# A finer first normalisation, a bias loaded element by element and a memset moved, in a two-layer attention and MLP kernel

## Chip, cores and metric

The kernel runs on one core of a Trainium2 chip. The metric is the device time of one execution in microseconds (us), measured several times; the median is quoted, with the lowest and highest. The profile is of one of these executions. Its span (first to last instruction) is about 2 us shorter than the device time. The "granted clock" is the share of its full clock at which TensorE was let run; 1.000 is all of it.

## The reference, cut to what matters

The program is two layers of attention and MLP on x of 2048 tokens by 1024 channels, in bf16. The biases b1 and b2 are the same in both layers.

```python
# attention: 32 heads of 32, each token looks at 8 keys, 2 apart (0, 2, ..., 14 tokens back)
x = x + attention(layernorm(x), wqkv, wo)      # wqkv: 1024 x 3072, wo: 1024 x 1024
x = x + gelu(layernorm(x) @ w1 + b1) @ w2 + b2 # w1: 1024 x 3584, w2: 3584 x 1024, b1: 3584
x = x + attention(layernorm(x), wqkv, wo)
x = x + gelu(layernorm(x) @ w1 + b1) @ w2 + b2
```

## The kernel before

Tokens are handled in four groups of 512 (4 tiles of 128). For each group the kernel computes queries, keys and values chunk by chunk on TensorE, with VectorE doing the attention products beside it. Order on TensorE is fixed by the program. Weights come through a pool of five 1 MB tiles; SyncE issues the weight loads and the DMA transposes of the normalised x in program order, and GpSimd issues a few others. "K(0)" below is the key phase of group 0 (units 8 to 15 of the first stage), and "V(0)" the value phase behind it.

The start: the first two x tiles are normalised and transposed on TensorE, and the first query matmuls need the transposed columns 0 to 255 of both.

```python
def norm(tt, parts=1):
    rstd = lnp.tile([P, 1], F32, name="rstd")
    vec.reciprocal(rstd[:], stds[tt][:])
    xn = lnp.tile([P, D], BF16, name="xn", bufs=3)
    for h in range(parts):
        cols = slice(h * D // parts, (h + 1) * D // parts)
        vec.tensor_scalar(out=xn[:, cols], in0=x[tt][:, cols], scalar1=mvs[tt][:, 0:1], scalar2=rstd[:],
                          op0=ALU.subtract, op1=ALU.mult)
    return xn

stats(0)
stats(1)
xn0 = norm(0)
xn1 = norm(1, 2)                       # 512 columns, then 512
transpose_on_pe(xn0, xa[0][:, 0, :, :], parts=[act.copy] * 4)
transpose_on_pe(xn1, xa[0][:, 1, :, :], parts=[vec.tensor_copy] * 2, k1=KD // 2)
transpose_on_pe(xn1, xa[0][:, 1, :, :], parts=[act.copy] * 2, k0=KD // 2)
# ... cut: statistics of the next tiles
```

The biases: b1 is wanted with its 3584 values spread over partitions (`b1T[p, j] = b1[j * 128 + p]`), for the ScalarE GELU. It is read as 28 rows of 128 and transposed on TensorE in K(0). b2 is read as one row of 2 KB, repeated on all 128 partitions.

```python
b1_rows = attp.tile([KF, P], BF16, name="abc")                      # KF = 28
pool.dma_start(b1_rows[:], B_b1.rearrange("(j p) -> j p", p=P))     # at the very start

def load_b2():
    pool.dma_start(b2bc[:], B_b2.unsqueeze(0).to_broadcast([P, D]))

def transpose_bias():
    ps = psum.tile([P, KF], BF16, name="acc", bufs=8)
    pe(nc.tensor.transpose(ps[:], b1_rows[:], ident[:KF, :KF]))
    act.copy(b1T[:], ps[:])
# ... cut
stage(gen_qkv(0, qk_next=early), sides=at(8, transpose_bias) + at(9, ln_stats_ahead, 2, NTT - 2)
      + at(11, ln_end) + at(14, load_b2))
q1 = gen_qkv(1, defer=True, qk_pool=early, mix=NCH // 2)
stage(q1, sides=at(0, gather, 0) + at(11, between, 0, 1) + at(11, hold) + each(av, 0, 12, 1))
```

`at(u, f)` calls f after unit u. `ln_end` normalises the last two tiles of group 2 and sends them through two DMA transposes; the SyncE queue then holds, in this order: the query weights of group 1 and the first half of its key weights, those two transposes, the second half of the key weights ("the second key-weight half" below), the value weights. The second half must take the buffer of V(0)'s first value-weight half.

## Time and profile before

| | before |
|---|---|
| device time, median of 3 (lowest to highest) | 1230.99 us (1230.79 to 1232.06) |
| profiled span | 1228.7 us |
| TensorE busy | 1223.1 us |
| waits of TensorE after 8.6 us | none |

The page gives busy time, share of the span and number of instructions of each engine (its part 1), and the shares of the chain of work that ended last, followed back from the last instruction (its part 4). PE is TensorE's matmuls, PEld its weight loads, DVE VectorE, ACT ScalarE, POOL GpSimd, SP SyncE.

```profile
PE 1223.1 (100%) x5771; PEld 632.5 (51%) x5771; DVE 862.1 (70%) x913; ACT 319.2 (26%) x515; POOL 108.7 (9%) x211
...
PE 99%; DVE 0%; DMA 0%; issue 0%
```

TensorE is the whole chain. The list of waits of TensorE (who waited for whom: total us, times, longest) says how little there is to take away:

```profile
PE acc L220 <- DVE xn L92: 1.5, 1, 1.5
PE acc L117 <- DVE big L92: 1.0, 1, 1.0
PE acc L117 <- DVE xnT L92: 0.2, 1, 0.2
```

All three lie in the first 8.6 us. In order of time (start us, length us, what), the chain shows the two places that the change aims at: the 12 transposes and the copy ahead of the first matmul, and at 25.32 the bias transpose.

```profile
7.12 0.93 PE acc L220 x12
...
8.08 0.30 DVE xnT L92
...
8.52 4.13 PE acc L117 x36
...
25.32 0.12 PE acc L181
```

The timeline (start us, length us, engine, line, operation, out<-in, and in brackets the idle time before and what ended it):

```profile
25.36 0.59 ACT L92 CAST kT<-acc 128x512 bf16<-128x512 f32 x1 [1.35 <-PE acc L117]
...
27.35 0.59 ACT L92 CAST kT<-acc 128x512 bf16<-128x512 f32 x1 [1.32 <-PE acc L117]
...
41.08 0.63 POOL L92 DMA_DIRECT2D b2bc<-in_B_b_dram  x1
...
43.50 9.31 SPq L92 DMA_TRANSPOSE xnT<-qT  x2
...
52.90 1.08 SPq L92 DMA_DIRECT2D wt<-in_A_wqkv_dram  x2
...
54.84 1.07 ACT L92 CAST qT<-acc 128x512 bf16<-128x512 f32 x2 [2.09 <-DMA xnT<-qT]
...
60.16 0.59 ACT L92 CAST kT<-acc 128x512 bf16<-128x512 f32 x1 [1.14 <-PE acc L117]
```

The two DMA transposes are landed by 54.84 (the query copy waits for them, because it reuses the memory that they read). The load at 52.90 is the second key-weight half; taken by itself, the trace gives its time from issue to landing:

```profile
DMA to landing us min/median/max: 5.6/5.6/5.6
```

So it lands at 52.9 + 5.6 = 58.5 us. TensorE wants it half a chunk after the four query chunks, near 59.3 us: about 0.8 us of slack. In windows (PE, PEld, DVE, ACT and POOL busy us, then the granted TensorE clock, the busy share of the DMA engines and GB/s), TensorE is full, and up to 60 us the DMA engines are full too. (Their share sums the times of all packets, and packets overlap, so it can exceed 1.)

```profile
50.00:55.00 5.00, 5.00 (x25) 3.31 (x24) 4.97 (x3) 1.70 (x5) 0.00 (x0) 1.00 1.20 197
55.00:60.00 5.00, 5.00 (x25) 3.34 (x24) 4.93 (x4) 2.09 (x4) 0.00 (x0) 1.00 1.00 377
60.00:65.00 5.00, 5.00 (x25) 3.33 (x24) 5.00 (x3) 1.76 (x3) 2.17 (x4) 1.00 0.32 122
```

A packet is one entry of the trace's DMA records: one piece moved by one engine.

### The profile page before, as it was taken

Reading aid. Unit: us, or ns where it says so; the run is one execution under the profiler, and the core shown is the slowest. Engines: PE = TensorE matmul, PEld = TensorE weight load, DVE = VectorE, ACT = ScalarE, POOL = GpSimd, SP = SyncE. Lnnn points to the kernel's source line nnn. Section 1 sums busy time; section 2 is a strip of 40 time slices with the busy share of each in tenths; the row PEclk is TensorE's granted clock in tenths of the full one; section 3 lists DMA queues with packets and bytes.
Section 4 is the critical chain, followed back from the end, with each engine's and each line's share of the span. In section 5 each row is a group of like instructions: output and inputs, shape, how many; then the busy total and the mean of one; then the engine's idle time right before and its main releaser. Section 6 shows DMA issues by size and latency. Waiting matters only on the chain.

```text
span 1228.7 us, 14007 instructions
## 1 busy us (share of the span) xinstructions
PE 1223.1 (100%) x5771; PEld 632.5 (51%) x5771; DVE 862.1 (70%) x913; ACT 319.2 (26%) x515; POOL 108.7 (9%) x211
## 2 busy tenths in 40 slices
PE   9999999999999999999999999999999999999999
PEld 7666544456444564446544465444654444444444
DVE  7999887998997999375993759937599797011001
ACT  5443253014310244202441024410244001400310
POOL 2310014010101101100001000000000002000000
PEclk9999999999999999999999999999999999999999
DMA  9954665766638645856557565576664568446441
GB/s 298 294 205 157 180 204 182 201 173 204 218 128 244 187 150 167 237 171 177 157 161 229 171 171 179 159 215 202 171 201 146 187 194 209 148 160 195 156 134 53
DMA packets 220031, 226.64 MB, mean 184 GB/s; under 512 B 68194, under 2 KB 187136, under 8 KB 217920
## 3 DMA queue, kind: packets, MB, share of 16 engines
q1 hardware_dynamic: 214704, 208.69, 56.7%
q0 software_dynamic: 5264, 17.06, 3.6%
q8 instruction: 45, 0.74, 0.3%
q14 instruction: 18, 0.15, 0.0%
HBM read 189.01 MB, written 4.19 MB: 157 GB/s over the span
## 4 chain that ended last, share of the span: by engine, by line
PE 99%; DVE 0%; DMA 0%; issue 0%
PE acc L117 99%; DMA x<-in_A_x_dram 0%; DVE stats L92 0%; PE acc L220 0%; DVE xn L92 0%; DVE x L92 0%; DVE mv L92 0%; DVE xnT L92 0%; PE acc L181 0%; DVE rstd L92 0%
## 5 line engine op out<-in xcount | busy, mean ns | idle before, releaser
L117 PE MATMUL acc<-xnT,wt 128*128 128x512 bf16 (+1 forms) x3392 | 720.5, 375 | 0.2 <-DVE xnT L92 0.2
L117 PEld LDWEIGHTS <-wt 128*128 128x128 bf16 x3392 | 400.7, 120 | 317.6 <-issue 0.3
L117 PE MATMUL acc<-wt,hT 128*128 128x512 bf16 (+1 forms) x1820 | 388.1, 376 | 0.0
L117 PEld LDWEIGHTS <-hT 128*128 128x128 bf16 x1820 | 178.1, 98 | 209.0
L92 DVE TENSOR_TENSOR big<-big 128x1024 bf16<-128x1024 bf16 (+2 forms) x184 | 244.9, 1360 | 2.2
L92 ACT ACTIVATE hT<-acc,b1T 128x512 bf16<-128x512 f32 x224 | 152.0, 688 | 322.2 <-PE acc L117 322.1
L92 DVE TENSOR_TENSOR big<-qT,kT 128x4096 bf16<-128x4096 bf16 x64 | 143.9, 2284 | 38.8 <-ACT kT L92 35.8
L92 DVE TENSOR_TENSOR big<-abc,vT 128x4096 bf16<-128x4096 bf16 x64 | 144.7, 2285 | 11.3 <-DMA abc<-a 9.2
L92 DVE TENSOR_TENSOR tmp<-acc,b2bc 128x512 f32<-128x512 f32 x56 | 38.6, 690 | 157.3 <-PE acc L117 154.3
L92 ACT CAST qT<-acc 128x512 bf16<-128x512 f32 (+1 forms) x72 | 38.2, 545 | 277.8 <-PE acc L117 275.7
L117 PE MATMUL acc<-wt,oT 128*128 128x512 bf16 x448 | 97.8, 379 | 0.0
L92 DVE BATCH_NORM_STATS2 stats<-x 128x6 f32<-128x512 bf16 x116 | 77.5, 682 | 6.1 <-DMA x<-in_A_x_dram 5.1
L117 PEld LDWEIGHTS <-oT 128*128 128x128 bf16 x448 | 43.9, 98 | 52.8
L92 DVE TENSOR_TENSOR x<-acc,big 128x512 bf16<-128x512 f32 (+1 forms) x9 | 5.7, 633 | 90.0 <-PE acc L117 90.0
L92 ACT CAST vT<-acc 128x512 bf16<-128x512 f32 x64 | 37.5, 586 | 100.8 <-PE acc L117 100.8
L92 POOL TENSOR_TENSOR rstd<-mv,eps_t 128x1 f32<-128x1 f32 x54 | 16.7, 310 | 530.1 <-DVE mv L92 530.1
L92 ACT CAST kT<-acc 128x512 bf16<-128x512 f32 x64 | 37.4, 585 | 64.6 <-PE acc L117 64.6
L92 DVE TENSOR_TENSOR x<-acc,x 128x512 bf16<-128x512 f32 x64 | 43.0, 672 | 4.6 <-PE acc L117 4.2
L92 DVE TENSOR_SCALAR xn<-x,mv,rstd 128x1024 bf16<-128x1024 bf16 (+1 forms) x53 | 28.6, 542 | 20.1 <-POOL rstd L92 19.7
L92 DVE TENSOR_TENSOR x<-tmp,x 128x512 bf16<-128x512 f32 x56 | 38.6, 690 | 1.4
L92 POOL DMA_DIRECT2D big<-big x24 | 13.3, 564 | 212.6 <-DVE big L92 212.5
L92 ACT ACT_TABLE_LOAD x17 | 21.8, 1283 | 36.6 <-DVE e L92 28.4
(64 smaller groups left out, 276.6 us busy)
## 6 DMA issues: line engine op xcount, KB each, us to landing
wt<-in_B_w_dram SPq DMA_DIRECT2D x56, 1024.0 KB, 5.7
wt<-in_B_w_dram SPq DMA_DIRECT2D x64, 896.0 KB, 4.9
wt<-in_A_wqkv_dram SPq DMA_DIRECT2D x46, 1024.0 KB, 5.6
wt<-in_A_wo_dram SPq DMA_DIRECT2D x16, 1024.0 KB, 5.1
abc<-a POOLq DMA_DIRECT2D x32, 256.0 KB, 5.1
big<-big POOLq DMA_DIRECT2D x24, 256.0 KB, 3.8
x<-in_A_x_dram SPq DMA_DIRECT2D x16, 256.0 KB, 7.1
out_dram<-x SPq DMA_DIRECT2D x31, 128.0 KB, 1.8
```

What stands on the lines that cost most here:

```text
L92: inst = f(*args, **kwargs)
L117: return pe(nc.tensor.matmul(*args, **kwargs))
```

## The change

Intent: let the first matmul start sooner (only 256 columns of the second tile have to be normalised and transposed first), take the bias transpose off TensorE by letting the DMA write b1 in transposed order with the cast to float32, and relieve GpSimd of one memset. The core of the diff:

```diff
+    vec.memset(zhalo[:], 0.0)
...
     def build_constants():
-        pool.memset(zhalo[:], 0.0)
...
-    b1_rows = attp.tile([KF, P], BF16, name="abc")
-    pool.dma_start(b1_rows[:], B_b1.rearrange("(j p) -> j p", p=P))
+    def load_b1():
+        pool.dma_start(b1T[:], B_b1.rearrange("(j p) -> p j", p=P))
...
-    def transpose_bias(): ...
...
-        def norm(tt, parts=1):
+        def norm(tt, bounds=(0, D)):
...
-            for h in range(parts):
-                cols = slice(h * D // parts, (h + 1) * D // parts)
+            for lo, hi in zip(bounds[:-1], bounds[1:]):
+                cols = slice(lo, hi)
...
-        xn1 = norm(1, 2)
+        xn1 = norm(1, (0, 2 * P, D))
-        transpose_on_pe(xn1, xa[0][:, 1, :, :], parts=[vec.tensor_copy] * 2, k1=KD // 2)
-        transpose_on_pe(xn1, xa[0][:, 1, :, :], parts=[act.copy] * 2, k0=KD // 2)
+        transpose_on_pe(xn1, xa[0][:, 1, :, :], parts=[vec.tensor_copy], k1=2)
+        transpose_on_pe(xn1, xa[0][:, 1, :, :], parts=[vec.tensor_copy] + [act.copy] * 2, k0=2)
...
-sides=at(8, transpose_bias) + at(9, ln_stats_ahead, 2, NTT - 2) + at(11, ln_end) + at(14, load_b2)
+sides=at(9, ln_stats_ahead, 2, NTT - 2) + at(11, ln_end) + at(13, load_b1) + at(14, load_b2)
```

More of the change, by code (lines that the diff above doesn't have):

```diff
@@ L170, in build_constants @@
         pool.dma_start(mask[0::NTT, :, :], first[:])
-    b1_rows = attp.tile([KF, P], BF16, name="abc")
-    pool.dma_start(b1_rows[:], B_b1.rearrange("(j p) -> j p", p=P))
+    def load_b1():
+        pool.dma_start(b1T[:], B_b1.rearrange("(j p) -> p j", p=P))
     def load_b2():
         pool.dma_start(b2bc[:], B_b2.unsqueeze(0).to_broadcast([P, D]))
-    def transpose_bias():
-        ps = psum.tile([P, KF], BF16, name="acc", bufs=8)
-        pe(nc.tensor.transpose(ps[:], b1_rows[:], ident[:KF, :KF]))
-        act.copy(b1T[:], ps[:])
     def ln_stats(t, mv=None, rstd=None):
@@ L629 @@
         load_x(1)
-        stage(gen_qkv(0, qk_next=early), sides=at(8, transpose_bias) + at(9, ln_stats_ahead, 2, NTT - 2) + at(11, ln_end) + at(14, load_b2))
+        stage(gen_qkv(0, qk_next=early), sides=at(9, ln_stats_ahead, 2, NTT - 2) + at(11, ln_end) + at(13, load_b1) + at(14, load_b2))
         q1 = gen_qkv(1, defer=True, qk_pool=early, mix=NCH // 2)
```

## The prediction

> **What bounds the kernel now.** The chain of waits is TensorE for 99% of the 1228.7 us span; TensorE is busy 1223.1 us. Its waits are three, all before 8.6 us: 1.5 us for the first normalised tile, 1.0 us for the warm-up data, 0.2 us for the transposed tile. From 8.52 us on it waits for nothing, so the change can gain only before 8.52 us or by removing TensorE work, and can lose by making TensorE wait.
>
> **Gain 1, start-up.** In the chain, 12 PE transposes (7.12 to 8.06 us) lead to VectorE's copy at 8.08, and that to the first matmul at 8.52. Eight are tile 0's; four are the second tile's first 512 columns, of which only two must now precede the first copy. In the timeline transposes issue about 0.065 us apart: 0.13 us saved. VectorE's second normalisation still ends near 7.91 us (estimated from 512 columns at 0.41 and 1024 at 0.55 us), so the copy can start near 7.95. The other six transposes run from 7.96 to about 8.36. The first matmul should start at 8.38 to 8.42.
>
> **Gain 2.** The bias transpose holds 0.12 us of the chain at 25.3 us; it goes, with an off-chain 0.19 us ScalarE copy.
>
> **No effect.** The zhalo memset took 0.21 us on GpSimd; VectorE is idle from 0.92 to 3.53 us. The early b1 load (7 KB) is negligible.
>
> **Cost: the new b1 load.** It moves 3584 elements of 2 bytes with a cast. The Trainium skill ("DMA: Bandwidth & Descriptors", Rules for kernel authors) says that a non-contiguous last dimension becomes one descriptor per element and that a cast must be issued from GpSimd; no run shows it yet. That is about 224 tiny packets per DMA engine. In the trace's packet records a 4-byte packet took 9 ns, a 256-byte one 18 ns: an estimated 2 to 4 us of all 16 engines, issued near 41 us, where the DMA share is about 1.0 (windows, 40 to 60 us). GpSimd must also produce the descriptors: perhaps 10 to 25 us, a guess.
>
> b1T is first read at 156 us. Three others have deadlines: the second key-weight half of group 1, issued at 52.9 behind two DMA transposes, wanted near 59.3, landing near 58 (slack about 1 us, the thinnest); gather(0) on the GpSimd queue, issued at 62.6, landing near 67, read at 71.0; behind it VectorE's attention of group 0, ready roughly 2 to 4 us before its output projection at 123.9. I expect the tiny packets to drain before 55 us: probably no stall.
>
> **Prediction.** 1230.99 - 0.12 - 0.12 = 1230.75 without a stall (about two chances in three); with a stall of 0.5 to 5 us otherwise, 1230.9 us overall, range 1230.0 to 1234.0. Faster by over 2%: 0.005; within 2%: 0.97; slower by over 2%: 0.025.
>
> **What would show it right.** First 256-column matmul near 8.40 us; no 28x28 transpose; TensorE's waits still all before 9 us; a GpSimd issue of b1T near 41 us longer than the 0.63 us of b2's; about 3600 more packets on the software queue; gather(0) issued by 63 us.
>
> **What would make it wrong.** A TensorE wait for weights at 59 to 62 us, or at the output projection near 124 us (gather(0) late, VectorE slipped). Or an unmoved first matmul: the six late transposes end last. A gain over 0.5 us would mean that the early b1 load had delayed the x tiles.

## More of the kernel before

The two key copies on ScalarE at 25.36 and 27.35 follow two chunks of eight matmuls; the bias transpose lies between them.

In the microsecond from 53 to 54 the DMA queues (packets, MB, share of 16 engines) held one entry, the transposes' 256-byte packets:

```profile
q1 hardware_dynamic: 1152, 0.29, 127.8%
```

## The result, and the profile after

| | before | after |
|---|---|---|
| device time, median of 6 (lowest to highest) | 1231.06 us (1230.79 to 1232.06) | 1235.63 us (1233.69 to 1237.22) |
| ratio, after over before | | 1.0036, 95% interval 1.0023 to 1.0049 |
| profiled span | 1228.7 us | 1231.5 us |
| mean granted clock over the six runs | 1.000 (in every later run listed) | 1.000, 0.999, 0.999, 0.997, 1.000, 0.998 |

Ratios are the mean time of one kernel's runs over that of the other's runs of the same rounds, so not quite the ratio of the medians quoted. The change made the kernel slower by some 4.6 us, well within 2%, but outside the predicted range. The profiled execution happens to be the quickest of the six (1233.69 us), so its loss of 2.8 us is the least of it.

The page after, parts 1 and 4 as above:

```profile
PE 1221.0 (99%) x5720; PEld 632.5 (51%) x5770; DVE 862.2 (70%) x914; ACT 318.8 (26%) x514; POOL 115.1 (9%) x210
...
PE 95%; DMA 2%; DVE 2%; issue 1%; SPq 0%; POOL 0%; DVEq 0%
```

The chain is no longer TensorE alone. (The smaller count of matmuls is of records missing from the trace; the weight loads fell by the one that was removed.) The list of waits names the newcomer at once:

```profile
PE acc L117 <- DMA wt<-in_A_wqkv_dram: 2.9, 1, 2.9
PE acc L117 <- DVE big L92: 1.0, 1, 1.0
PE acc L213 <- DVE xn L92: 0.9, 1, 0.9
```

The timeline after, cut to the lines that answer to those shown before:

```profile
7.22 1.35 PE L213 MATMUL acc<-ident,xn 128*128 128x128 bf16 x16 [0.92 <-DVE xn L92]
8.43 4.19 PE L117 MATMUL acc<-xnT,wt 128*128 128x256 bf16 x36
...
25.33 0.58 ACT L92 CAST kT<-acc 128x512 bf16<-128x512 f32 x1 [1.35 <-PE acc L117]
27.06 0.58 ACT L92 CAST kT<-acc 128x512 bf16<-128x512 f32 x1 [1.14 <-PE acc L117]
...
40.85 1.65 POOL L92 DMA_DIRECT2D b1T<-in_B_b_dram  x1
...
42.50 0.59 POOL L92 DMA_DIRECT2D b2bc<-in_B_b_dram  x1
...
43.34 8.27 SPq L92 DMA_TRANSPOSE xnT<-qT  x2
...
51.70 1.09 SPq L92 DMA_DIRECT2D wt<-in_A_wqkv_dram  x2
...
59.37 2.05 ACT L92 CAST qT<-acc 128x512 bf16<-128x512 f32 x4 [6.92 <-DMA xnT<-qT]
...
61.84 13.39 PE L117 MATMUL acc<-xnT,wt 128*128 128x512 bf16 x61 [2.87 <-DMA wt<-in_A_wqkv_dram]
...
62.96 0.59 ACT L92 CAST kT<-acc 128x512 bf16<-128x512 f32 x1 [1.54 <-PE acc L117]
```

Three copies on ScalarE measure where the time went. The first key copy of K(0) moved from 25.36 to 25.33 us: in this pair of profiles the start-up part had gained 0.03 us by then. The second moved from 27.35 to 27.06: the distance between the two fell from 1.99 to 1.73 us, so the bias transpose had cost TensorE 0.26 us (in load_only, below, the distance is 1.73 us too, and in start_only, which kept the bias transpose, 2.00). The first key copy of group 1 moved from 60.16 to 62.96: 2.80 us late, which is also the difference of the spans. Everything is decided by 63 us; the stall cost 2.80 + 0.29 = 3.1 us, of which the wait itself is 2.87.

The second key-weight half was issued 1.2 us earlier than before (51.70 against 52.90), yet took almost twice as long to land:

```profile
DMA to landing us min/median/max: 10.1/10.1/10.1
```

It landed at 61.8 us. It stands in the SyncE queue behind the two DMA transposes, and these were landed only at 59.37 instead of 54.84 us. In the same microsecond, 53 to 54, the queues show why:

```profile
q1 hardware_dynamic: 383, 0.10, 125.7%
q0 software_dynamic: 385, 0.00, 76.8%
```

The transposes moved 383 packets instead of 1152, and beside them passed 385 packets with hardly a byte in them: b1's elements, on GpSimd's queue. One for one. (This is the last part of the transposes. Before it they differed little: from the first transpose packet to 53 us, 787 packets in 2.4 us in the kernel before, 1095 in 3.7 us in the changed one.) The windows show the hole in TensorE, and in the first line a DMA share that is up and a GB/s that is down by half:

```profile
50.00:55.00 5.00, 5.00 (x25) 3.34 (x24) 4.97 (x4) 1.25 (x4) 0.00 (x0) 1.00 2.00 109
55.00:60.00 5.00, 3.97 (x19) 2.37 (x17) 4.93 (x4) 0.63 (x2) 0.00 (x0) 1.00 1.38 222
60.00:65.00 5.00, 3.16 (x15) 2.14 (x16) 3.29 (x2) 2.32 (x5) 2.16 (x4) 1.00 0.98 364
```

The trace's packet records add a second suspect. Before, b2's load (64 packets of 4096 bytes) went through from 45.1 to 47.2 us. After, it stood behind the elements in GpSimd's queue and went through from 54.2 to 58.5 us, on the end of the transposes; single packets of it took up to 1.47 us, against at most 0.44 us before.

### The profile page after: what moved, and what is told of

It reads as the page before. It is cut to its first block, busy times and chain, and to the rows that moved or that the text cites. A ratio compares the mean times of both kernels' runs of the same rounds, so it can differ in the third digit from the quotient of the medians. Undisturbed runs are those within 1.5% of the kernel's fastest.

```text
span 1231.5 us, 13954 instructions
## 1 busy us (share of the span) xinstructions
PE 1221.0 (99%) x5720; PEld 632.5 (51%) x5770; DVE 862.2 (70%) x914; ACT 318.8 (26%) x514; POOL 115.1 (9%) x210
## 3 DMA queue, kind: packets, MB, share of 16 engines
q0 software_dynamic: 8832, 17.07, 4.3%
## 4 chain that ended last, share of the span: by engine, by line
PE 95%; DMA 2%; DVE 2%; issue 1%; SPq 0%; POOL 0%; DVEq 0%
PE acc L117 95%; DMA wt<-in_A_wqkv_dram 1%; DVE big L92 1%; DMA x<-in_A_x_dram 1%; SPq L92 0%; DVE stats L92 0%; DVE qT L92 0%; POOL rstd L92 0%; DVE mv L92 0%; DVE x L92 0%; DVEq L92 0%
## 5 line engine op out<-in xcount | busy, mean ns | idle before, releaser
L92 DVE TENSOR_SCALAR xn<-x,mv,rstd 128x1024 bf16<-128x1024 bf16 (+2 forms) x53 | 28.6, 540 | 20.0 <-POOL rstd L92 19.8
```

Of the source, the lines that this page charges most:

```text
L92: inst = f(*args, **kwargs)
```

## The experiments

Theory A: the 3584 element packets alternate, packet by packet, with SyncE's queue on the DMA engines, draw out the transposes, and so delay the second key-weight half. Rival B: any cast load by GpSimd at this moment, ahead of b2's, does it, whatever its packets. Rival C: the new start-up shifts everything by 0.3 us and that uses up the slack. More theories came as runs fell out otherwise than expected. All runs gave correct results except where said.

Medians are of 4 to 6 runs; "before" is the kernel before in the same rounds. "Wait" is TensorE's total wait for key or query weights in the profiled execution.

| run | median us (lowest to highest) | before | ratio, 95% interval | wait us |
|---|---|---|---|---|
| load_only | 1236.03 (1232.71 to 1236.45) | 1231.22 | 1.0033 (1.0020 to 1.0045) | 3.7 |
| start_only | 1231.05 (1230.62 to 1231.91) | 1231.22 | 0.9999 (0.9985 to 1.0012) | none |
| load_late | 1230.70 (1230.52 to 1231.52) | 1231.22 | 0.9997 (0.9984 to 1.0009) | none |
| contiguous | 1230.79 (1230.41 to 1231.14) | 1231.22 | 0.9995 (0.9983 to 1.0008) | none |
| half_load | 1231.80 (1230.79 to 1232.40) | 1231.21 | 1.0005 (0.9992 to 1.0017) | none |
| double_load | 1232.29 (1231.76 to 1233.11) | 1231.21 | 1.0009 (0.9996 to 1.0023) | 1.8 |
| keys_first | 1237.34 (1236.42 to 1239.96) | 1231.21 | 1.0056 (1.0044 to 1.0069) | 0.2, and 5.6 for ScalarE |
| sync_queue | 1232.51 (1231.96 to 1234.18) | 1231.21 | 1.0015 (0.9999 to 1.0030) | 1.7 |
| b2_first | 1233.09 (1232.48 to 1234.50) | 1230.98 | 1.0019 (1.0006 to 1.0031) | 3.3 |
| b2_late | 1232.23 (1230.52 to 1232.42) | 1230.98 | 1.0006 (0.9993 to 1.0018) | 1.5 |
| b2_shifted | 1230.68 (1230.44 to 1232.40) | 1230.98 | 0.9999 (0.9985 to 1.0013) | none |
| after_again | 1237.10 (1235.27 to 1238.20) | 1230.98 | 1.0046 (1.0033 to 1.0059) | 4.8 |
| b2_rows | 1234.04 (1232.06 to 1237.14) | 1231.04 | 1.0031 (1.0019 to 1.0044) | 1.3 |
| b2_shifted_more | 1231.40 (1230.46 to 1232.15) | 1231.04 | 1.0001 (0.9988 to 1.0015) | 0.6 |

### Which part of the change: load_only and start_only

load_only is the kernel before with the new load alone; start_only is the changed kernel with the old b1 path put back.

```diff
 load_only, against the kernel before:
-    b1_rows = ...; pool.dma_start(b1_rows[:], ...); def transpose_bias(): ...
+    def load_b1(): pool.dma_start(b1T[:], B_b1.rearrange("(j p) -> p j", p=P))
-sides=at(8, transpose_bias) + ... + at(14, load_b2)
+sides=... + at(13, load_b1) + at(14, load_b2)
 start_only, against the changed kernel: these lines the other way round
```

> The kernel before with the new b1 load alone (element DMA at its new place, no bias transpose; 512+512 normalisation and the GpSimd memset kept). Theory A (the 3584 two-byte packets share the DMA engines with the transposes and the second key-weight half, which lands late): slower, about 1234 to 1237 us, one TensorE wait of 2.5 to 7 us for key weights near 59 us, and a gain of about 0.26 us near 25 us from the missing bias transpose. Rival C (the start-up reordering shifts everything, and that is what collides): about 1230.8 us and no such wait.

> The changed kernel with the old b1 path put back (28-row load at the start, bias transpose on TensorE); the 256+768 normalisation and the VectorE memset kept. Theory A: no TensorE wait after 9 us, time equal to before within 0.15 us (1230.9 to 1231.1), since the start-up part gained only about 0.03 us by 15 us in the traces. Rival C: 1234 us or more, with a wait for weights near 59 us.

load_only measured 1236.03 us, all of the loss; start_only 1231.05 us, no loss and no wait after 9 us. Rival C falls. load_only's profile is of a slower execution than the one seen so far (1236.11 us), and so it shows the other half of the cost. Its list of waits, the line for weights:

```profile
PE acc L117 <- DMA wt<-in_A_wqkv_dram: 3.7, 1, 3.7
```

and its windows behind the wait:

```profile
55.00:60.00 5.00, 3.82 (x18) 2.29 (x16) 4.93 (x4) 0.00 (x0) 0.00 (x0) 1.00 1.66 181
60.00:65.00 5.00, 2.48 (x8) 1.19 (x9) 2.55 (x2) 2.64 (x5) 2.15 (x4) 0.82 1.04 387
65.00:70.00 5.00, 5.00 (x21) 2.91 (x20) 2.44 (x2) 1.17 (x2) 0.00 (x0) 0.84 0.34 135
```

The granted clock is 0.82 and 0.84 in two windows of 5 us. That is one spell of 3.41 us at half clock in the trace's record of the clock, and it costs (0.18 + 0.16) x 5 = 1.7 us on top of the wait (the record has it begin at 63.17 us, 0.65 us after the wait had ended): TensorE is "busy" from 65 to 70 us with 21 matmuls where 25 fit. The Trainium skill ("TensorE: Matmul & The Clock Gate", Why this matters for your kernels) asks for no idle gaps over about 3 us between matmul bursts, because an idle window brings the clock down to half; its Part 1 gives that window as 3413 ns. Waits of 2.87 us (the changed kernel's profile) and 3.0 us (b2_first's) left the clock at 1.00, and waits of 3.69 and 4.57 us brought one spell of 3.41 us each (keys_first's, of 5.58 us, brought 6.83 us). So the length at which a wait begins to cost clock lies between 3.0 and 3.7 us in these runs; they do not place it closer.

### How many packets, and when: load_late and contiguous

load_late issues the same element load about 45 us later, behind the GpSimd DMAs of group 0's attention; nothing changes its order on the other engines. contiguous loads at the changed kernel's place, with the same cast and bytes, but 128 runs of 28 elements; the bias order is wrong on purpose (the biases are so small that the comparison passed).

```diff
 load_late:
-sides=... + at(13, load_b1) + at(14, load_b2)          # group 0
+sides=... + at(14, load_b2)
-... + at(11, hold) + each(av, 0, 12, 1))              # group 1
+... + at(11, hold) + at(11, load_b1) + each(av, 0, 12, 1))
 contiguous:
-        pool.dma_start(b1T[:], B_b1.rearrange("(j p) -> p j", p=P))
+        pool.dma_start(b1T[:], B_b1.rearrange("(p j) -> p j", p=P))
```

> The changed kernel with the same element load issued some 45 us later, behind the last GpSimd DMA of group 0's attention, when the DMA engines are mostly idle; order on TensorE, VectorE, ScalarE and SyncE unchanged. Theory A: no TensorE wait after 9 us; 1230.7 us, that is 0.3 us under before (0.26 from the bias transpose, 0.03 from start-up). Rival C (the 0.3 us shift itself uses up the slack): a wait for weights near 59 us remains, 1233 us or more.

> The changed kernel with b1 read at the same moment by the same GpSimd cast load of the same 7 KB, but in contiguous order: 128 runs of 28 elements instead of 3584 single elements. The biases land in the wrong order on purpose (they are so small that the comparison may pass). Theory A (number of packets): no wait after 9 us, 1230.7 us. Rival B (a cast load from GpSimd at that moment, ahead of b2's, whatever its packets): the wait near 59 us remains and the time is 1233 to 1237 us.

Both came out as theory A has it: 1230.70 and 1230.79 us and no wait after 9 us. Rival B falls: 128 packets at the same moment, from the same engine, with the same cast, do no harm. The number of packets and what is beside them is what counts. The time from issue to landing of b1's load, in the changed kernel and then in load_late:

```profile
DMA to landing us min/median/max: 17.5/17.5/17.5
```

```profile
DMA to landing us min/median/max: 5.5/5.5/5.5
```

In load_late the packet records show all 3584 elements gone in some 2.2 us (88.2 to 90.4 us), at up to 2158 in one microsecond, with the SyncE queue empty. In the changed kernel they took from 45.9 to about 56 us.

load_late is the version that the experiments point to: it keeps what the change gains. Its profiled span is 1228.4 us against 1228.7, the 0.3 us that the two copies in K(0) showed, though the first of these copies scatters by more than that from one profile to the next (25.11 to 26.09 us). Its median is 0.5 us under before's, but the interval of the ratio holds 1, so the gain is seen in the traces and not settled by the timing. Against the changed kernel it is about 5 us faster in the medians.

### Half and double the dose: half_load and double_load

```diff
 half_load: bias columns 0 to 13 at the changed kernel's place, 14 to 27 at the late place
+    def load_b1(j0, j1):
+        pool.dma_start(b1T[:, j0:j1], B_b1[j0 * P:j1 * P].rearrange("(j p) -> p j", p=P))
 double_load:
         pool.dma_start(b1T[:], B_b1.rearrange("(j p) -> p j", p=P))
+        pool.dma_start(b1_again[:], B_b1.rearrange("(j p) -> p j", p=P))
```

> The changed kernel with 14 of the 28 bias columns loaded at the changed kernel's place (1792 element packets) and the other 14 at the late place. Theory A with packet-by-packet alternation (in the changed kernel's trace an element packet took 22 ns and made its partner of the other queue 14 ns longer, so about 36 ns per pair per engine; 112 pairs fewer): the second key-weight half lands near 60 us, a wait of 0 to 1.5 us, no reduced clock, 1230.7 to 1232.3 us. If the stall came from a fixed cost of having the load there at all, it stays at 3 us or more.

> The changed kernel with the element load issued twice (the second into an unused tile): 7168 element packets. Theory A with alternation: each packet of the other queue is followed by at most one element packet, and most packets ahead of the key weights already had a partner; only the 32 key-weight packets per engine gain one, so the wait grows by about 1 us, to 4 to 5.5 us, and 1236.5 to 1239 us. Rival D (what counts is the total DMA time of the elements, about 36 ns each on 16 engines, 8 us more): the wait grows by 6 us or more, 1241 us or more.

half_load fits: 1231.8 us, and no wait in its profile, which is however that of the quickest of its five runs (1230.79 us). double_load is a miss for both theories: with twice the packets the kernel was faster than with one dose, 1232.29 us and a wait of 1.8 us. The packet records say what else had changed: with 7168 elements ahead of it in GpSimd's queue, b2's load went through only from 63.5 us, after the key weights, instead of at 54 to 58 us. So theory A was incomplete. Theory E: two things act together, the elements' alternation, and b2's packets that the elements push into the end of the transposes.

### b2's part: b2_first, b2_late, b2_shifted, b2_shifted_more, b2_rows

b2_first swaps the two bias loads. b2_late leaves the elements and moves b2's load to the late place. b2_shifted and b2_shifted_more are load_late (no elements about) with b2's load held back by a small GpSimd copy that waits for a value of V(0), so that its packets fall at 51.8 to 53.1 us and at 53.8 to 55.7 us. b2_rows is the changed kernel with b2's load reading 128 different rows.

```diff
 b2_first:
-... + at(13, load_b1) + at(14, load_b2)
+... + at(13, load_b2) + at(14, load_b1)
 b2_late:
-... + at(13, load_b1) + at(14, load_b2)
+... + at(13, load_b1)                                  # and at(11, load_b2) in the stage of group 1
 b2_shifted, against load_late (b2_shifted_more: chunk 6, unit 22):
-... + at(14, load_b2)
+... + at(20, load_b2)
     def load_b2():
+        gate = smp.tile([P, 1], F32, name="gate")
+        pool.tensor_copy(gate[:], st[0]["vT"][:, 4, HALO:HALO + 1])
 b2_rows (wrong bias on purpose; the comparison passed):
-        pool.dma_start(b2bc[:], B_b2.unsqueeze(0).to_broadcast([P, D]))
+        pool.dma_start(b2bc[:], B_w1[0:P, 0:D])
```

> The changed kernel with the two bias loads swapped: b2's load (64 or so packets of 4096 bytes, all reading the same 2 KB) is issued first, b1's elements behind it. New theory E (two causes: the elements' alternation, and b2's packets, pushed by the elements from 45-47 us to 54-58 us, into the last transposes, where single ones took up to 1.3 us): b2's packets are back at 45 to 47 us, the transposes end about 56 us as in the doubled run, the wait for the key weights is 0.8 to 2.2 us, no half clock, 1231.4 to 1233 us. Theory A (alternation alone, 7 to 8 us of element time behind everything): unchanged against the changed kernel, a wait of 2.5 us or more and 1234 to 1237 us.

> The changed kernel with b2's load moved to the late place (some 45 us later), the element load where the change put it. Theory E: only the alternation is left; also 2 us less of b2 traffic near 45 us, so a wait of 0 to 1.8 us, 1230.8 to 1232.6 us. Theory A: a wait of 2.5 us or more, 1234 to 1237 us.

> The late-load kernel (no element packets before 88 us), with b2's load held back until a value of group 0 is written (near 47 us), so that its packets fall near 51 to 54 us among the transposes. Theory E in its strong form (b2's packets alone harm the transposes): the transposes and the key weights are 0.5 to 2 us later than in the late-load kernel, a wait of 0.2 to 1.5 us for key weights, 1231 to 1232.5 us. If b2's packets harm only together with elements: no wait, 1230.7 us.

> The changed kernel with b2's load reading 128 different rows of 2 KB (from w1, so the bias is wrong on purpose and the output too) instead of one row of 2 KB 128 times. Same queue, same place behind b1's elements, same bytes. Theory F (b2's packets are harmful because all engines read the same 2 KB): packets take about 160 ns each, the key weights' wait falls to the 1.2 to 2 us of the elements alone, 1231.5 to 1233 us. If it is enough that 64 packets of 4096 bytes stand behind the elements: a wait of 2.5 to 5 us remains, 1234 to 1238 us.

> As the earlier kernel with the late element load and b2 held back, but held about 3.5 us longer, so that b2's packets fall near 54 to 57 us, where they fell in the changed kernel, on the end of the transposes and the start of the key weights, with no element packets about. If b2's packets at that moment do harm by themselves: the key weights land 0.5 us or more later than in the late-load kernel and a wait of 0.3 to 2 us appears, 1231 to 1232.7 us. If they harm only after elements have drawn out the transposes: no wait over 0.3 us, 1230.7 us.

With b2's load out of the way, the elements alone cost 1.25 us in the median (1232.23 against 1230.98 us; the interval of the ratio holds 1, so the timing alone does not settle it), and the wait in b2_late's profile is less than a third of that of the changed kernel in the same rounds. b2_late's line, and that of after_again:

```profile
PE acc L117 <- DMA wt<-in_A_wqkv_dram: 1.5, 2, 1.2
```

```profile
PE acc L117 <- DMA wt<-in_A_wqkv_dram: 4.8, 2, 4.6
```

b2_first brought the time down from 1237.1 to 1233.1 us in the same rounds by changing only the order of two loads, so most of the loss needs b2's load behind the elements. It is a near miss all the same: its median is at the upper edge of what was expected, and its profile has a wait of 3.3 us where at most 2.2 was expected; in that execution the transposes ended only at 58.7 us, and the key weights were issued at 55.06 (SyncE's issues had run more than a microsecond behind the changed kernel's since 36 us).

b2_shifted (1230.68 us, no wait) and b2_shifted_more (1231.40 us, a wait of 0.6 us) show that b2's packets by themselves, at about the times where they fell in the changed kernel, cost little: none, and about 0.4 us, neither clear of noise. But without elements the transposes end earlier, at 52.6 and 53.9 us, so b2's packets met only their last microsecond or less. So it takes both.

The packet records say the same without the timing's noise. From the first packet of the two transposes to the end of the last, one execution each: 3.0 to 3.9 us without elements beside them (before, start_only, load_late, contiguous, b2_shifted, b2_shifted_more); 4.9 us with half of the elements (half_load); 5.8, 5.9 and 6.6 us with all of them but b2's packets elsewhere (b2_late, double_load, b2_first); 8.2, 8.3 and 8.5 us with both (load_only, the changed kernel, after_again).

b2_rows was to tell whether b2's packets harm because they all read the same 2 KB. Its six runs spread from 1232.06 to 1237.14 us, and its interval overlaps that of the changed kernel, although the profiled execution, the quickest of the six, had a wait of 1.3 us only; there the transposes took 6.7 us and ended at 55.75 us, so b2's packets (54.8 to 56.9 us) hardly met them. This is unclear; the question stays open.

### Where the harm goes: keys_first and sync_queue

keys_first moves the two DMA transposes behind the second key-weight half, the elements staying. sync_queue sends the elements through SyncE's own queue, into a bf16 tile that VectorE casts later.

```diff
 keys_first:
-... + at(11, ln_end) + ...                             # group 0
+sides=at(0, ln_end) + at(0, gather, 0) + ...           # group 1
 sync_queue:
     def load_b1():
-        pool.dma_start(b1T[:], B_b1.rearrange("(j p) -> p j", p=P))
+        sp.dma_start(b1h[:], B_b1.rearrange("(j p) -> p j", p=P))
+    def cast_b1():
+        vec.tensor_copy(b1T[:], b1h[:])
```

> The changed kernel with the element load where it is, but the last two DMA transposes of K(0) moved behind the second key-weight half in the SyncE queue. Theory A, with the transposes as the victims that hold up the weights behind them: the weights are no longer behind 128 slowed 256-byte packets per engine and land by 57 us; no wait after 9 us, about 1230.8 us (0.3 us to 1 us more is possible where VectorE's order moved). If the weight stream itself were the victim, a wait of 2 us or more would remain.

> The changed kernel with the same 3584 elements issued from SyncE, so in the same queue as weights and transposes, into a bf16 tile that VectorE casts later; it stands ahead of group 1's query weights. Theory A (the harm is alternation with another queue): in one queue the elements are served one after the other (9 ns each in the late run, about 2 us in all) and then out of the way: no wait near 59 us, 1230.7 to 1231.5 us. If an element packet costs some 36 ns wherever it stands, about 8 us are added ahead of the weights: a wait of 3 us or more for group 1's query weights near 52 us, 1234 us or more.

keys_first is a miss in time, 1237.34 us, and its edit did more than was meant: VectorE reached the two normalisations so late that the transposes went out at 61.9 us, and the query copies of group 1, which must wait for them, held up TensorE for want of free tiles in PSUM, the memory that TensorE writes to. Its list of waits, the two lines that matter:

```profile
PE acc L117 <- ACT qT L92: 5.6, 1, 5.6
...
PE acc L117 <- DMA wt<-in_A_wqkv_dram: 0.2, 1, 0.2
```

The wait for weights is down to 0.2 us with all 3584 elements in place, which fits theory A: the key weights came late because of the transposes ahead of them. But the run does not show it: another wait took over, and with little in SyncE's queue from 50.5 to 53 us, the elements were gone by 52.9 us (1232 and 1282 of them in single microseconds), before most of the key weights moved.

sync_queue is a miss too: a wait of 1.7 us and 1232.51 us instead of no wait. What was expected of the elements came true: in one queue they did not alternate, and the packet records have all 3584 pass from 40.8 to 42.8 us, at 9 ns each. Its DMA queues from 41 to 45 us:

```profile
q1 hardware_dynamic: 3416, 0.06, 56.2%
```

Of the 3416 packets all but a few are elements, gone by 42.8 us; then SyncE's queue moved next to nothing until 44.2 us. What had not been expected: the weight load behind the elements took SyncE 3.64 us to issue, against 0.38 us for the first weight load before, and so the weights came that much later. Its median is still 3.1 us under the changed kernel's of the first rounds; how much of that is the queue and how much is b2's load, which stayed early here, this run does not separate.

### The changed kernel once more: after_again

> The changed kernel once more, unedited, for its scatter and for another profile. Theory: one wait of 2.5 to 4.5 us for the key weights near 59 us in every run, and in those runs whose mean granted clock is below 1.000 one or two windows of about 3.4 us at half clock behind the wait, 1.7 us lost in each. 1235.6 us median, 1233 to 1237.5 us.

The unedited kernel came out a little slower than expected: 1237.10 us, up to 1238.20, a wait of 4.8 us in the profile (4.57 us of it in one piece), one spell of 3.41 us at half clock behind it. All five runs had a mean clock below 1.000, and in the first six the two with 1.000 were the two quickest (1233.69 and 1234.30 us). The scatter of the changed kernel is thus mostly that of one wait around 3 to 5 us, on either side of the length at which the clock goes down.

## Why the prediction was wrong

- **What bounds the kernel, and where it could lose.** Right. TensorE waited for nothing, and the loss is a TensorE wait for weights in the very place named as having the thinnest slack (59 to 62 us named, 58.97 to 61.84 measured).
- **Gain 1, start-up: 0.12 us.** Not too large at the first matmul: from the first PE transpose to it the profiles have 1.40 us before and in load_only, which keeps the old start-up, and 1.21 us after (1.21 to 1.22 in start_only, load_late and contiguous), a gain of 0.18 us. The first matmul moved only from 8.52 to 8.43 us because the transposes began 0.10 us later in this execution. How much of it lasts is not settled: the first key copy stands at 25.36 us before and 25.19 in load_only, and anywhere from 25.11 to 26.09 us in the profiles with the new start-up. start_only's timing shows no gain that can be told from noise.
- **Gain 2, bias transpose: 0.12 us.** Right in kind, half of what it was: 0.26 us between two key copies. The chain's 0.12 us is the piece that one instruction holds, not what TensorE loses around it. The two gains together, 0.29 us in this pair of profiles, come close to the 0.24 predicted; as the first copy scatters, that is partly luck.
- **No effect of the memset.** Nothing contradicts it: start_only contains it and shows no loss.
- **Cost of the b1 load: the step that failed.** The prediction put the elements at "an estimated 2 to 4 us of all 16 engines", expected them "to drain before 55 us: probably no stall", and allowed for "0.5 to 5 us" in one case of three. The number of packets was right (the software queue went from 5264 to 8832 packets), and so is the estimate for elements that run alone: 2.2 us in load_late. (With some luck: the 9 ns were those of other 4-byte packets; the elements themselves took 25 ns in the median there, several at once.) But that estimate took the length of a tiny packet for its cost. Beside another queue each element cost a turn of that queue. From 53 to 54 us the transposes fell from 1152 to 383 packets; the 2048-byte weight packets only from about 198 to 163 in a microsecond. A queue of small packets is what such alternation hurts most, and two DMA transposes of 256-byte packets stood right ahead of the weights. The elements did not drain before 55 us but near 56, the transposes' last packet ended at 57.6 instead of 54.2 us, and the key weights landed at 61.8 instead of 58.5. The elements alone cost 1.25 us in the median (b2_late).
- **What the prediction did not have at all.** First, b2's load behind the elements: it was pushed from 45 us to 54 to 58 us, onto the end of the transposes. The two together cost 4.6 to 6.1 us, each alone 1.25 and about 0.4 us or nothing (neither of these last two clear of noise). Second, the price of a wait: waits of 3.69 and 4.57 us also halved TensorE's clock for 3.41 us, 1.7 us more. The Trainium skill ("TensorE: Matmul & The Clock Gate", Why this matters for your kernels) warns of it, and the prediction added up waits as if they cost their own length.
- **GpSimd's issue of the load.** Longer than the 0.63 us of b2's, as was asked, and without effect: it took 1.65 us, and gather(0) was issued at 62.17 us, in time.

What stays open: counted from load_late (0.52 us under its before), elements alone cost 1.25 + 0.52 = 1.8 us, b2's shifted load alone 0.36 + 0.52 = 0.9 us, and a spell of half clock 1.7 us. That makes 4.4 us; the changed kernel lost 4.57 + 0.52 = 5.1 and 6.12 + 0.52 = 6.6 us in its two sets. The remaining 0.7 to 2.2 us (an estimate: medians whose intervals are some 1.5 us wide to either side), why b2's packets are slower just there (up to 1.5 us for one), and whether reading the same 2 KB has to do with it, were not shown.

## What to carry to other kernels

Count a scattered load in packets, not bytes, and look at what shares the DMA engines while they pass: another queue's packets, above all small ones, may give up every second turn, and whatever stands behind them in their queue comes late. Put such a load where the DMA engines are idle and no deadline is near (here, 45 us later, with the whole loss gone), or make it few packets. When a kernel is bound by TensorE and its weights land with less than a microsecond to spare, price a possible wait as the wait plus, if it is long, a spell of half clock (here, 1.7 us after waits of 3.69 and 4.57 us and nothing after waits up to 3.0 us).

## What the Trainium skill lacked or had wrong

- "DMA: Bandwidth & Descriptors", Rules for kernel authors: one descriptor per element of a non-contiguous last dimension. Agrees: 5264 to 8832 packets on the software queue, which is 3584 elements less the 16 packets of the old load. Lacking: what such a load costs by its surroundings, 17.5 us from issue to landing beside a full queue and 5.5 us beside an empty one, for the same data.
- The same page, Queues, rings and completion order: each DMA engine takes turns between queues packet by packet. Agrees: 383 against 385 packets from 53 to 54 us. Lacking: the consequence that a queue of 256-byte packets at full rate drops to a third (1152 to 383 in that microsecond) beside a queue of single elements, where one of 2048-byte packets loses about a sixth (198 to 163).
- The same page, Anatomy of one DMA: the fit of 2.0 us plus bytes over 436 GB/s for a GpSimd load has no term for the number of packets. For the 14 KB that b1's load writes it gives an estimate of 2.03 us; element by element the load took 5.4 us at best (b2_shifted_more) and 17.5 us in the changed kernel. The number of packets is not the whole of it: in 128 runs, beside a busy queue, it took 6.1 us (contiguous).
- "TensorE: Matmul & The Clock Gate", Why this matters for your kernels: idle gaps over about 3 us bring the clock to half. Agrees: waits of 2.87 and 3.0 us did not, 3.69 and 4.57 us did, for 3.41 us each time, 1.7 us of time lost.
- No page tells how slow single packets of a load like b2's can become: those of 4096 bytes took up to 1.47 us in the changed kernel, against 0.16 us at best and 0.44 us at most before. That they all read one row is not shown to be the reason: from 128 different rows (b2_rows) they took up to 0.87 us, and with no element about (b2_shifted_more) up to 0.99 us.
